# Transposes of batch 1 later in their step, and TensorE's order as written in every chunk

## The chip, the cores and the metric

The kernel runs on one core of a Trainium2 chip. The metric is the device time of one execution in microseconds (us), as the median of several runs. A change within 0.3% of the time before, some 3 us, is about what repeated runs cannot tell from no change.

## The reference, cut to what matters

Attention with a window of 32 positions (half of the heads plain, half with dilation 4) is followed by a rank-32 mix over the sequence and a two-layer ReLU network, each with a residual.

```python
scores = scale * np.matmul(q, k.transpose(0, 1, 3, 2))      # q, k, v: (8, 8, 576, 64)
scores = np.where(masks[None], scores, -1e9)
attn = np.exp(scores - np.max(scores, axis=-1, keepdims=True))
attn = attn / (np.sum(attn, axis=-1, keepdims=True) + 1e-09)
x = np.matmul(attn, v).transpose(0, 2, 1, 3).reshape(8, 576, 512)
...
h = x.transpose(0, 2, 1) @ U @ V                            # rank 32
u = x + h.transpose(0, 2, 1)
return u + np.maximum(u @ w_ch1, 0.0) @ w_ch2               # 512 -> 2048 -> 512
```

## The kernel before, in words

The 4608 tokens are 36 tiles of 128. The two-layer network runs over twelve *chunks* of tiles: chunk 0 has four tiles, chunk 1 two, chunks 2 to 11 three each. In a chunk a loop runs over 16 *units* f, each a 128-wide part of the hidden layer. `layer1(f)` (L853) multiplies the split weights `w1h`, `w1l` with the split inputs `uth`, `utl` into the PSUM tile `ph`, 12 matmuls; ScalarE takes `hh` out of it with the ReLU (L858), VectorE takes the remainder `hl` (L859). `layer2(f)` (L877) adds `hh` times `w2h`, `hh` times `w2l` and `hl` times `w2h` into one `acc` per tile, and runs one unit behind: layer1(f), layer2(f-1), layer1(f+1), ... In the last unit layer2(14) and layer2(15) follow each other. At a chunk's end VectorE adds `acc` to `x` (L913), and `out` is stored.

The attention of the batches is woven into this. A batch has nine *groups* g (batch 1 has g = 9 to 17, the last batch ends with g = 71), and each is a *step*: `pre` multiplies the probabilities of g-2 with v (`product`, tile `pv`, L402), makes the scores of g (`scores`, tiles `s`, L362) and normalizes `pv` into `x` or `xp` on VectorE (`place`, L432). Then come four `soften` (mask and maximum on VectorE, L373; exponential on ScalarE, L377). `post` transposes the probabilities (`turn`): for g < 18 with four TensorE transposes into the PSUM tile `ptp` (L382) and a VectorE copy into `pt` (L388), for the later ones with eight VectorE transposes (L394). `product` issues 8 instructions and `scores` 8; each shows as two passes in the trace, so 16 and 16. After a batch follow `t_rest` (tile `t`, L482) and five `mix_rest` (tile `m`, L504). The tiles `s`, `pv`, `ptp`, `t` and `m` share three PSUM buffers (tag `ps`), given out in the order of the code, so `ptp`, which follows `pv`, `s`, `s`, takes the buffer of that step's `pv` and waits until `place` has read it.

When each piece is issued is set by `queue`: pairs of a position (in units of three tiles) and a call; `slot()`, called after every few matmuls of the network, issues whatever is due. Batch 1 is due in chunk 0, where the weights are also unpacked from 64-bit values (`weight_step`, on all engines but TensorE).

What order the engines then get is another matter. Through chunk 0, and again from the last unit of chunk 11, the block `order = tc.manual_schedule(engines=ORDERED)` keeps all five engines in the order of the code. In between a scheduler with a time model of its own chooses each engine's order, and it may move any instruction ahead of one that it expects to wait.

Of the kernel before, what the change touches and what calls it, by code (L numbers as in the profile page):

```python
# [81 lines left out]
STEP0 = 0.012  # L82
STEP1 = 0.075
SPREAD_AT = 0.5
AFTER = (0.86, 0.90, 0.98, 1.02, 1.06, 1.10, 1.14)
LO2 = 1.31
HI2 = 2.45
# [50 lines left out]
def attention_moe_kernel(ctx: ExitStack, tc: tile.TileContext, qk, vv, masks, ident, ut, vt, uv, w1, w2, out):  # L138
# [196 lines left out]
    def load_v(g, i):  # L335
        if (g, 1, i) in loaded:
            return
        if g < NGB:
            t = early.tile([P, 2, UNITS, VW], F32, tag="v0", name=f"v{g}", bufs=NGB)
            nc.sync.dma_start(out=t, in_=vv[g])  # L340
            loaded[g, 1, 0] = t[:, 0]
            loaded[g, 1, 1] = t[:, 1]
        else:
            t = work.tile([P, UNITS, VW], F32, tag="v", name=f"v{g}_{i}", bufs=4)
            nc.sync.dma_start(out=t, in_=vv[g][:, i])
            loaded[g, 1, i] = t
# [240 lines left out]
    def attention_steps(b):  # L587
        held = {}
        turned = set()
        attn = []  # L590
        for s in range(NGB + LAG):
            g = NGB * b + s

            def pre(s=s, g=g):
                if b >= SPLIT and 0 < s <= NGB:
                    load_v(g - 1, 0)
                    load_v(g - 1, 1)
                if s < NGB and g + 2 < (NGB * SPLIT if b < SPLIT else NG):
                    load_q(g + 2)
                if s >= LAG:  # L600
                    pv = product(g - LAG, held.pop(g - LAG))
                if s < NGB:
                    scores(g)
                if s >= LAG:
                    place(g - LAG, pv)
                if b < SPLIT and LAG <= s < NGB:
                    load_v(g, 0)
                    load_v(g, 1)

            def post(s=s, g=g):  # L610
                late = g - (NGB * b < PE_T)
                if late in state and late not in turned:
                    turned.add(late)
                    held[late] = turn(late, state.pop(late)[0])

            units = [lambda u=u, g=g: soften(g, u) for u in range(UNITS if s < NGB else 0)]
            if b < SPLIT:
                attn.append([lambda pre=pre, units=units, post=post: (pre(), [x() for x in units], post())])
            else:
                attn.append([pre] + units + [post])  # L620
        return attn
# [111 lines left out]
    def batch_items(b):  # L733
        attn = attention_steps(b)
        n = len(batch_parts(b))
        after = [lambda: t_rest(b), lambda: t_sum(b)] + [lambda i=i: mix_rest(b, i) for i in range(n)]
        if b < SPLIT:
            timed = [(STEP0 + STEP1 * i, x) for i, step in enumerate(attn) for x in step]
            timed += [(STEP0 + STEP1 * (i + SPREAD_AT), lambda g=NGB * b + i - LAG: g in scatter and spread_rows(g))
                      for i in range(LAG, len(attn))]  # L740
            timed += list(zip(AFTER, after))
            return sorted(timed, key=lambda e: e[0])
        timed = []
        for i, step in enumerate(attn):
            timed += [(i, step[0])] + [(i + UNIT0 + (UNIT1 - UNIT0) * u / len(step[1:-1]), x) for u, x in enumerate(step[1:-1])] + [(i + POST_AT, step[-1])]
        timed += [(len(attn) + m * TAIL, x) for m, x in enumerate(after)]
        end = len(attn) + len(after) * TAIL
        return [(t / end, x) for t, x in sorted(timed, key=lambda e: e[0])]
# [43 lines left out]
    def after_first():  # L792
        early_open.close()
        make_w(F_MID, F_LAST, None)
# [34 lines left out]
    for c, tiles in enumerate(CHUNKS):  # L829
        slots = [0]  # L830
        nt = len(tiles)
        uh, ul = (e[:, :, 0:nt * P] for e in uts.pop(c))
        acc = [psum.tile([P, DM], F32, tag="acc" if i < CT else "ph", name=f"acc{c}_{i}", bufs=3 if i < CT else 2)
               for i in range(nt)]
        ht = {}

        def slot():
            pos = (tiles[0] + nt * slots[0] / ((nt + 3) * FC - 3)) / CT
            slots[0] += 1
            while queue and queue[0][0] <= pos:  # L840
                queue.pop(0)[1]()

        def layer1(f):
            assert place_of[f, 0] in finished
            ph = psum.tile([P, CTOK], F32, tag="ph", name=f"ph{c}_{f}", bufs=2)[:, 0:nt * P]
            w1h, w1l = held_w[f][0:2]
            ks = (2, 3, 0, 1) if c == f == 0 else range(KC)
            terms = [(w1h, uh), (w1l, uh), (w1h, ul)]
            if c == 0 and f > 0:
                terms = [terms[0], terms[2], terms[1]]  # L850
            seq = [(w, u, k) for w, u in terms for k in ks]
            for n, (w, u, k) in enumerate(seq):
                nc.tensor.matmul(ph, lhsT=w[:, k, :], rhs=u[:, k, :], start=(n == 0), stop=(n == len(seq) - 1))  # L853
                if n % KC == KC - 1 and n < len(seq) - 1:
                    slot()
            hh = work.tile([P, CTOK], F32R, tag="hh", name=f"hh{c}_{f}", bufs=2)[:, 0:nt * P]
            hl = work.tile([P, CTOK], F32R, tag="hl", name=f"hl{c}_{f}", bufs=2)[:, 0:nt * P]
            nc.scalar.activation(out=hh, in_=ph, func=AF.Relu)  # L858
            nc.vector.scalar_tensor_tensor(out=hl, in0=ph, scalar=0.0, in1=hh.bitcast(F32),  # L859
                                           op0=ALU.max, op1=ALU.subtract)  # L860
            ht[f] = (hh, hl)

        def layer2(f):
            assert place_of[f, 1] in finished
            hh, hl = ht.pop(f)
            w2h, w2l = held_w[f][2:4]
            terms = [(hh, w2h), (hh, w2l), (hl, w2h)]
            seq = [(i, n, term) for i in range(nt) for n, term in enumerate(terms)]
            if c == 0:
                terms = [terms[0], terms[2], terms[1]]  # L870
                seq = [(i, n, term) for n, term in enumerate(terms) for i in range(nt)]
            every = slice(0, DM)
            seq = [e + (every,) for e in seq]
            if c == NCHUNK - 1 and f == FC - 1:
                seq[-3:] = [e[:3] + (slice(k * HALF_D, (k + 1) * HALF_D),) for k in range(2) for e in seq[-3:]]
            for m, (i, n, (h, w), cs) in enumerate(seq):
                nc.tensor.matmul(acc[i][:, cs], lhsT=h[:, i * P:(i + 1) * P], rhs=w[:, cs],  # L877
                                 start=(f == 0 and n == 0), stop=(f == FC - 1 and n == 2 and cs.stop == DM))
                if f < FC - 1 and m % 3 == 2 and m < len(seq) - 1:
                    slot()  # L880

        more = list(CHUNKS[c + 1]) if c + 1 < NCHUNK else []
        for f in range(FC):
            if c == 0 and f == F_MID - 1:
                after_first()
            if c == 0:
                weight_step()
            if c == NCHUNK - 1 and f == FC - 1:
                order = tc.manual_schedule(engines=ORDERED)
                order.__enter__()  # L890
            layer1(f)
            if f < FC - 1:
                slot()
            else:
                for t in more[0:2]:
                    transp(t)
            if c == 0:
                weight_step()
            if f > 0:
                layer2(f - 1)  # L900
                if f < FC - 1:
                    slot()
        for t in more[2:]:
            transp(t)
        layer2(FC - 1)
        if c == 0:
            order.__exit__(None, None, None)
        for i, t in enumerate(tiles):
            x = xt.pop(t)
            n = 2 if t == NTILE - 1 else 1  # L910
            for h in range(n):
                cs = slice(h * DM // n, (h + 1) * DM // n)
                nc.vector.tensor_tensor(out=x[:, cs], in0=acc[i][:, cs], in1=x[:, cs], op=ALU.add)  # L913
                nc.sync.dma_start(out=out[t * P:(t + 1) * P, cs], in_=x[:, cs])
        if c == NCHUNK - 1:
            order.__exit__(None, None, None)


def lay_out(q, k, v, U, V, w1, w2):
# [74 lines left out]
```

## Time and profile before

| | |
|---|---|
| runs, median (lowest to highest) | 993.83 us (991.52 to 993.94) |
| profiled execution | 995.63 us |
| its span, first to last instruction | 993.8 us |
| granted TensorE clock, mean over the span | 0.993 |
| TensorE busy | 970.6 us |
| VectorE / ScalarE / GpSimd busy | 501.1 / 267.8 / 73.9 us |

The span is what the trace covers; 1.8 us lie around it. The profiled execution is itself 1.8 us above the median of the three runs. Busy time of TensorE counts from a matmul's start to its modelled end, and matmuls overlap, so that what a matmul costs is read from start to start.

### The profile page before, as it was taken

What the parts mean: (1) busy time and instruction counts of PE and PEld (TensorE: products, weight loads), DVE (VectorE), ACT (ScalarE), POOL (GpSimd) and SP (SyncE); (2) the same over time, 40 slices, a digit from 0 to 9 for tenths busy, and PEclk for the clock granted to TensorE, in tenths of its full rate; (3) what the DMA queues carried; (4) which work ended last, traced back from release to release, by engine and by line L of the source; (5) the groups of instructions that cost most, each with busy time, mean ns of one, the idle gap of its engine ahead of it and who ended that gap; (6) DMA issues with size and microseconds to landing.
All of it is one profiled execution on the core that took longest, in us unless ns stands there. A gap on an engine that the chain in (4) does not pass through costs nothing.

```text
span 993.8 us, 17434 instructions
## 1 busy us (share of the span) xinstructions
PE 970.6 (98%) x6672; PEld 815.3 (82%) x6672; DVE 501.1 (50%) x1686; ACT 267.8 (27%) x669; POOL 73.9 (7%) x67
## 2 busy tenths in 40 slices
PE   8968899999999999999999999999999999999998
PEld 5656677888888888888888888888888888999997
DVE  5646776664657446563356634664536644211211
ACT  7645563221222213222122212221212311111110
POOL 1544453000000000000000000000000000000000
PEclk9979999999999999999999999999999999999999
DMA  9556545322334132321323312332313303100000
GB/s 327 184 181 207 164 155 158 115 79 67 89 95 119 45 76 86 114 74 33 85 72 102 101 27 71 104 112 63 86 40 95 97 11 83 56 1 1 33 1 32
DMA packets 76995, 90.44 MB, mean 91 GB/s; under 512 B 9904, under 2 KB 55280, under 8 KB 76912
## 3 DMA queue, kind: packets, MB, share of 16 engines
q1 hardware_dynamic: 76912, 89.32, 30.1%
q8 instruction: 53, 0.87, 0.4%
q14 instruction: 30, 0.25, 0.1%
HBM read 67.26 MB, written 17.89 MB: 86 GB/s over the span
## 4 chain that ended last, share of the span: by engine, by line
PE 91%; DVE 3%; issue 2%; POOL 2%; DMA 1%; ACT 1%; SPq 0%; DVEq 0%; POOLq 0%
PE ph L853 39%; PE acc L877 39%; PE pv L402 5%; PE s L362 4%; PE t L482 1%; DVE v L204 1%; PE ptp L382 1%; PE m L504 1%; POOL v L204 1%; DMA k<-qk 1%; POOL w1l L211 1%; POOL w2l L211 0%; ACT hh L858 0%; DMA zd<-z 0%; DMA spare<-xp 0%
## 5 line engine op out<-in xcount | busy, mean ns | idle before, releaser
L859 DVE SCALAR_TENSOR_TENSOR hl<-ph,hh 128x384 fp32r<-128x384 f32 (+2 forms) x192 | 106.7, 556 | 269.1 <-ACT hh L858 267.5
L877 PE MATMUL acc<-w2h,hh 128*128 128x512 f32 x577 | 225.3, 403 | 0.6 <-ACT raw L198 0.6
L858 ACT ACTIVATE hh<-ph 128x384 fp32r<-128x384 f32 (+2 forms) x192 | 94.0, 490 | 480.6 <-PE ph L853 473.5
L877 PE MATMUL acc<-w2l,hh 128*128 128x512 f32 x577 | 220.5, 395 | 0.0
L877 PE MATMUL acc<-w2h,hl 128*128 128x512 f32 x577 | 209.4, 397 | 0.0
L853 PE MATMUL ph<-uth,w1h 128*128 128x384 f32 (+2 forms) x768 | 171.0, 342 | 1.3 <-DVE hl L859 1.3
L853 PE MATMUL ph<-uth,w1l 128*128 128x384 f32 (+2 forms) x768 | 167.4, 339 | 0.0
L853 PE MATMUL ph<-utl,w1h 128*128 128x384 f32 (+2 forms) x768 | 166.1, 338 | 0.0
L853 PEld LDWEIGHTS ph<-uth,w1h 128*128 128x128 f32 x768 | 136.4, 189 | 21.5 <-DVE hl L859 2.2
L394 DVE STREAM_TRANSPOSE pt<-p 32x128 f32<-32x128 f32 x432 | 130.4, 302 | 36.9 <-ACT p L377 31.4
L853 PEld LDWEIGHTS ph<-utl,w1h 128*128 128x128 f32 x768 | 134.8, 189 | 3.6
L853 PEld LDWEIGHTS ph<-uth,w1l 128*128 128x128 f32 x768 | 133.1, 188 | 4.7
L377 ACT ACTIVATE p<-p,nmax 128x96 f32<-128x96 f32 x288 | 86.0, 365 | 172.9 <-DVE nmax L373 172.7
L877 PEld LDWEIGHTS acc<-w2h,hh 128*128 128x128 f32 x577 | 108.0, 188 | 24.9 <-issue 1.2
L877 PEld LDWEIGHTS acc<-w2h,hl 128*128 128x128 f32 x577 | 108.0, 189 | 23.8
L877 PEld LDWEIGHTS acc<-w2l,hh 128*128 128x128 f32 x577 | 109.4, 190 | 17.2 <-issue 0.4
L373 DVE CUSTOM_DVE_ANT_0 p<-s,mask 128x96 f32<-128x96 f32 x288 | 57.5, 251 | 26.6 <-PE s L362 26.1
L402 PEld LDWEIGHTS pv<-v,pt 96*64 96x64 f32 x1152 | 44.2, 137 | 30.0 <-issue 26.7
L402 PE MATMUL pv<-v,pt 96*64 96x65 f32 x1152 | 59.0, 230 | 0.0
L362 PE MATMUL s<-k 64*64 64x96 f32 x1152 | 49.1, 256 | 2.1 <-DMA k<-qk 1.0
L362 PEld LDWEIGHTS s<-k 64*64 64x64 f32 x1152 | 31.3, 132 | 17.7 <-issue 11.3
L408 DVE TENSOR_SCALAR ssum<-pv 128x4 f32<-128x4 f32 x72 | 11.3, 157 | 60.3 <-PE pv L402 60.1
(69 smaller groups left out, 494.4 us busy)
## 6 DMA issues: line engine op xcount, KB each, us to landing
k<-qk SPq DMA_DIRECT2D x64, 288.0 KB, 3.2
v<-vv SPq DMA_DIRECT2D x126, 130.0 KB, 2.2
raw<-w SPq DMA_DIRECT2D x25, 512.0 KB, 3.9
out<-x SPq DMA_DIRECT2D x35, 256.0 KB, 2.2
zd<-z SPq DMA_DIRECT2D x120, 64.0 KB, 1.9
xt<-zd SPq DMA_DIRECT2D x30, 256.0 KB, 2.8
raw<-w SPq DMA_DIRECT2D x14, 256.0 KB, 3.1
x<-xp SPq DMA_DIRECT2D x84, 32.0 KB, 1.9
```

Of the source, the lines that this page charges most:

```text
L204: eng.tensor_tensor(out=vi[:, cs], in0=vi[:, cs], in1=lo, op=ALU.add)
L211: eng.tensor_tensor(out=l, in0=v, in1=h.bitcast(F32), op=ALU.subtract)
L362: nc.tensor.matmul(sp[r][i * QB:(i + 1) * QB, a, :], lhsT=qk_sb[rs, a, i * QB:(i + 1) * QB], rhs=qk_sb[rs, a, P + i * off:P + i * off + KB ...
L373: nc.vector.tensor_tensor_reduce(out=p_sb[:, u], in0=sp[u % 2][:, u // 2], in1=mask_sb[:, kind], scale=-1.0 / 8.0, scalar=3.0e38, op0=ALU. ...
L377: nc.scalar.activation(out=p_sb[:, u], in_=p_sb[:, u], func=AF.Exp, bias=nmax[:, u:u + 1], scale=-1.0)
L394: nc.vector.transpose(out=pt[ks, :, rs], in_=p_sb[rs, :, ks])
L402: nc.tensor.matmul(pv[rs, u, :], lhsT=pt[:, u, rs], rhs=loaded[g, 1, i][0:KB, u, :], start=True, stop=True)
L408: nc.vector.tensor_scalar(out=ssum, in0=pv[:, :, D], scalar1=1e-9, scalar2=None, op0=ALU.add)
L853: nc.tensor.matmul(ph, lhsT=w[:, k, :], rhs=u[:, k, :], start=(n == 0), stop=(n == len(seq) - 1))
L858: nc.scalar.activation(out=hh, in_=ph, func=AF.Relu)
L859: nc.vector.scalar_tensor_tensor(out=hl, in0=ph, scalar=0.0, in1=hh.bitcast(F32), op0=ALU.max, op1=ALU.subtract)
L877: nc.tensor.matmul(acc[i][:, cs], lhsT=h[:, i * P:(i + 1) * P], rhs=w[:, cs], start=(f == 0 and n == 0), stop=(f == FC - 1 and n == 2 and ...
```

## The change

Two things change. In batches 0 and 1 (in effect batch 1) a step is no longer one call that issues `pre`, `soften` and `post` together: `post`, with the four transposes and their copy, is due 0.4 of a step later than the rest. And from the end of chunk 0 to the end of the kernel TensorE alone keeps the order of the code, in a second `manual_schedule` block; VectorE, ScalarE and the DMA queue are still left to the scheduler there, and get another order in places since TensorE's is another.

```diff
+BACK_AT = 0.4
...
             if b < SPLIT:
-                attn.append([lambda pre=pre, units=units, post=post: (pre(), [x() for x in units], post())])
+                attn.append([lambda pre=pre, units=units: (pre(), [x() for x in units]), post])
...
-            timed = [(STEP0 + STEP1 * i, x) for i, step in enumerate(attn) for x in step]
+            timed = [(STEP0 + STEP1 * (i + BACK_AT * n), x) for i, step in enumerate(attn) for n, x in enumerate(step)]
...
         if c == 0:
             order.__exit__(None, None, None)
+            bursts = tc.manual_schedule(engines={mybir.EngineType.PE})
+            bursts.__enter__()
...
         if c == NCHUNK - 1:
             order.__exit__(None, None, None)
+            bursts.__exit__(None, None, None)
```

Names in the rows below carry the group, chunk or unit first (`s36`: scores of group 36; `acc3_0`, `hh3_13`: tile 0 of chunk 3, unit 13 of chunk 3) and a running number last.

TensorE in chunk 0, at the transposes of group 11, in the kernel before:

```order
L362 MATMUL s12_0_919<-k12_727 64x96 x2
L362 MATMUL s12_1_920<-k12_727 64x96 x2
L362 MATMUL s12_0_919<-k12_727 64x96 x2
L362 MATMUL s12_1_920<-k12_727 64x96 x2
L382 MATMUL ptp11_948<-id_sb_72,p11_829 96x128 x4
L877 MATMUL acc0_3_625<-w2h_0_83,hh0_2_788 128x512
L877 MATMUL acc0_0_622<-w2h_0_83,hl0_2_789 128x512
```

and in the changed one:

```order
L363 MATMUL s12_0_919<-k12_727 64x96 x2
L363 MATMUL s12_1_920<-k12_727 64x96 x2
L363 MATMUL s12_0_919<-k12_727 64x96 x2
L363 MATMUL s12_1_920<-k12_727 64x96 x2
L878 MATMUL acc0_3_625<-w2h_0_83,hh0_2_788 128x512
L878 MATMUL acc0_0_622<-w2h_0_83,hl0_2_789 128x512
L878 MATMUL acc0_1_623<-w2h_0_83,hl0_2_789 128x512
L878 MATMUL acc0_2_624<-w2h_0_83,hl0_2_789 128x512
L878 MATMUL acc0_3_625<-w2h_0_83,hl0_2_789 128x512
L878 MATMUL acc0_0_622<-w2l_0_84,hh0_2_788 128x512
L383 MATMUL ptp11_956<-id_sb_72,p11_829 96x128 x4
L878 MATMUL acc0_1_623<-w2l_0_84,hh0_2_788 128x512
```

Six matmuls of 512 columns now stand between the scores of group 12 and the transposes of group 11, where none stood.

TensorE near the end of chunk 3, at the scores of group 36, before:

```order
L853 MATMUL ph3_14_4186<-utl3_3548,w1h_13_1697 128x384 x4
L362 MATMUL s36_0_4208<-k36_3688 64x96
L877 MATMUL acc3_0_3587<-w2h_13_1699,hh3_13_4173 128x512
L877 MATMUL acc3_0_3587<-w2l_13_1700,hh3_13_4173 128x512
L362 MATMUL s36_1_4209<-k36_3688 64x96
L877 MATMUL acc3_0_3587<-w2h_13_1699,hl3_13_4174 128x512
L362 MATMUL s36_1_4209<-k36_3688 64x96
L362 MATMUL s36_0_4208<-k36_3688 64x96 x2
L362 MATMUL s36_1_4209<-k36_3688 64x96 x2
L877 MATMUL acc3_1_3588<-w2h_13_1699,hh3_13_4173 128x512
```

and after:

```order
L854 MATMUL ph3_14_4188<-utl3_3550,w1h_13_1697 128x384 x4
L878 MATMUL acc3_0_3589<-w2h_13_1699,hh3_13_4175 128x512
L878 MATMUL acc3_0_3589<-w2l_13_1700,hh3_13_4175 128x512
L878 MATMUL acc3_0_3589<-w2h_13_1699,hl3_13_4176 128x512
L363 MATMUL s36_0_4210<-k36_3690 64x96 x2
L363 MATMUL s36_1_4211<-k36_3690 64x96 x2
L363 MATMUL s36_0_4210<-k36_3690 64x96 x2
L363 MATMUL s36_1_4211<-k36_3690 64x96 x2
L878 MATMUL acc3_1_3590<-w2h_13_1699,hh3_13_4175 128x512
```

The eight matmuls of the scores stood in three pieces here (and one more stood 25 rows earlier, behind the first layer of unit 12); now they stand together, behind the three matmuls of `acc3_0`.

TensorE at the passage from chunk 3 to chunk 4, before:

```order
L853 MATMUL ph4_0_4294<-uth4_4247,w1h_0_81 128x384 x2
L877 MATMUL acc3_0_3587<-w2h_13_1699,hh3_15_4243 128x512
L877 MATMUL acc3_0_3587<-w2l_13_1700,hh3_15_4243 128x512
L877 MATMUL acc3_1_3588<-w2h_13_1699,hh3_15_4243 128x512
L877 MATMUL acc3_1_3588<-w2l_13_1700,hh3_15_4243 128x512
L877 MATMUL acc3_2_3589<-w2h_13_1699,hh3_15_4243 128x512
L877 MATMUL acc3_2_3589<-w2l_13_1700,hh3_15_4243 128x512
L853 MATMUL ph4_0_4294<-uth4_4247,w1h_0_81 128x384 x2
L853 MATMUL ph4_0_4294<-uth4_4247,w1l_0_82 128x384 x3
L877 MATMUL acc3_0_3587<-w2h_13_1699,hl3_15_4244 128x512
```

and after:

```order
L878 MATMUL acc3_2_3591<-w2h_13_1699,hl3_14_4202 128x512
L878 MATMUL acc3_0_3589<-w2h_13_1699,hh3_15_4245 128x512
L878 MATMUL acc3_0_3589<-w2l_13_1700,hh3_15_4245 128x512
L878 MATMUL acc3_0_3589<-w2h_13_1699,hl3_15_4246 128x512
L878 MATMUL acc3_1_3590<-w2h_13_1699,hh3_15_4245 128x512
L878 MATMUL acc3_1_3590<-w2l_13_1700,hh3_15_4245 128x512
L878 MATMUL acc3_1_3590<-w2h_13_1699,hl3_15_4246 128x512
L878 MATMUL acc3_2_3591<-w2h_13_1699,hh3_15_4245 128x512
L878 MATMUL acc3_2_3591<-w2l_13_1700,hh3_15_4245 128x512
L878 MATMUL acc3_2_3591<-w2h_13_1699,hl3_15_4246 128x512
L854 MATMUL ph4_0_4296<-uth4_4249,w1h_0_81 128x384 x4
```

The second layer of the last unit stood behind half of chunk 4's first `ph`, its products with `hl` last; now it follows the second layer of unit 14 at once, and the first product with `hl` is its third matmul.

Counted over all of TensorE's order behind chunk 0, the pieces of `pv` and `s` matmuls that stand between matmuls of the network go from 119 to 66: 42 whole bursts (8 `pv`, then 8 `s`), 12 of `pv` alone and 12 of `s` alone. Those of `t` go from 8 to 6. The `m` stand singly or in pairs before, singly after. What is computed, and the count of every instruction, stays the same.

## Rows read from the trace of the kernel before

**Rows 1.** Busy time of each engine by stretch; its first line names the columns.

```profile
core 0: us, PE busy (x) PEld busy (x) DVE busy (x) ACT busy (x) POOL busy (x), PEclk, DMA share, GB/s
...
36.00:165.00 129.00, 113.04 (x728) 87.70 (x725) 84.09 (x215) 67.88 (x155) 64.97 (x55) 0.95 0.55 175
165.00:860.00 695.00, 695.00 (x4870) 588.25 (x4869) 371.79 (x1315) 158.10 (x416) 0.00 (x0) 1.00 0.28 80
...
55.00:62.00 7.00, 5.91 (x17) 4.81 (x18) 2.60 (x14) 2.84 (x7) 2.69 (x2) 0.51 0.66 218
68.70:72.10 3.40, 3.40 (x10) 2.63 (x9) 1.02 (x2) 2.60 (x8) 1.85 (x2) 0.51 0.18 43
92.60:96.00 3.40, 3.40 (x11) 2.80 (x10) 1.20 (x7) 1.17 (x4) 1.35 (x2) 0.50 0.59 161
```

**Rows 2.** Waits of TensorE from 36 to 165 us: total, times, longest.

```profile
PE ptp L382 <- DVE xp L432: 9.6, 4, 5.1
PE ptp L382 <- DVE x L432: 1.9, 2, 1.2
PE ptp L382 <- ACT raw L198: 1.7, 1, 1.7
PE ph L853 <- DVE hl L859: 1.3, 2, 0.9
```

**Rows 3.** TensorE's timeline at the two longest stalls: start, us, instruction, [idle before].

```profile
56.09 1.06 PE L382 MATMUL ptp<-id_sb,p 128*96 128x128 f32 x4 [5.07 <-DVE xp L432]
68.11 0.61 PE L382 MATMUL ptp<-id_sb,p 128*96 128x128 f32 x4 [2.78 <-DVE xp L432]
```

**Rows 4.** VectorE's timeline just ahead of the first of them.

```profile
55.52 0.42 DVE L432 TENSOR_TENSOR xp<-pv,ssum 128x256 f32<-128x256 f32 x1
```

**Rows 5.** TensorE's timeline around an undivided burst.

```profile
273.81 0.39 PE L877 MATMUL acc<-w2h,hl 128*128 128x512 f32 x1
274.13 0.69 PE L402 MATMUL pv<-v,pt 96*64 96x65 f32 x16
274.75 0.56 PE L362 MATMUL s<-k 64*64 64x96 f32 x16
275.24 0.96 PE L853 MATMUL ph<-uth,w1h 128*128 128x384 f32 x4
```

**Rows 6.** TensorE's timeline around three pieces: the first, one midway, the last.

```profile
166.55 0.64 PE L853 MATMUL ph<-uth,w1h 128*128 128x256 f32 x4
167.11 0.55 PE L362 MATMUL s<-k 64*64 64x96 f32 x8
167.59 0.62 PE L853 MATMUL ph<-uth,w1l 128*128 128x256 f32 x3
...
266.45 0.86 PE L853 MATMUL ph<-utl,w1h 128*128 128x384 f32 x4
267.24 0.56 PE L362 MATMUL s<-k 64*64 64x96 f32 x16
267.73 0.50 PE L877 MATMUL acc<-w2h,hh 128*128 128x512 f32 x1
...
811.61 0.68 PE L853 MATMUL ph<-utl,w1h 128*128 128x384 f32 x3
812.22 0.69 PE L402 MATMUL pv<-v,pt 96*64 96x65 f32 x16
812.84 0.50 PE L877 MATMUL acc<-w2h,hh 128*128 128x512 f32 x1
813.18 0.40 PE L877 MATMUL acc<-w2l,hh 128*128 128x512 f32 x1
```

**Rows 7.** TensorE's timeline at the end of chunk 3.

```profile
380.37 0.39 PE L877 MATMUL acc<-w2h,hh 128*128 128x512 f32 x1
380.60 0.40 PE L877 MATMUL acc<-w2l,hh 128*128 128x512 f32 x1
```

**Rows 8.** VectorE's timeline there.

```profile
382.65 0.55 DVE L859 SCALAR_TENSOR_TENSOR hl<-ph,hh 128x384 fp32r<-128x384 f32 x1
```

## The prediction

> **What bounds the kernel now.** I read the busy time by stretch first. From 165 to 860 us, chunks 1 to 9, TensorE is busy for 695.00 of 695 us at the full clock [rows 1], and the view of waits shows no wait of TensorE at all in that stretch. So there the time is the sum of what TensorE issues, from start to start, and nothing else counts. Chunk 0 is different: between 36 and 165 us TensorE is busy for 113.04 of 129 us, and VectorE for 84.09 [rows 1]. The waits of that stretch name one instruction: the transposes `ptp` stand idle for 9.6 + 1.9 + 1.7 = 13.2 us, mostly for the `xp` or `x` that `place` writes on VectorE [rows 2]. The two longest are 5.07 and 2.78 us [rows 3]; in the first, `place` ends at 55.52 + 0.42 = 55.94 and `ptp` starts at 56.09 [rows 3, 4]. The clock is at its lower level, 1.2 GHz (0.51, 0.51, 0.50 granted), in three stretches, each begun behind one of these stalls: about 6.8, 3.4 and 3.4 us [rows 1].
>
> **What a piece of attention costs between wide matmuls.** Two 512-column matmuls start 0.23 us apart [rows 7]; by the ratio of columns that is 0.17 for 384 and 0.115 for 256. An undivided burst of 16 `pv` and 16 `s` passes lies between the matmul at 273.81 and the one at 275.24: 1.43, less the 0.23 that the first takes anyway, is 1.20 us [rows 5]. The matmul behind a piece is also late in being followed: 813.18 - 812.84 = 0.34 instead of 0.23, 0.11 more [rows 6]. I add it to every piece: a whole burst is 1.31. `pv` alone: 812.84 - 811.61 - 3 x 0.17 = 0.71, with the 0.11 0.82 us. The 16 `s` passes alone: 267.73 - 266.45 - 4 x 0.17 = 0.59, so 0.70. Half of them: 167.59 - 166.55 - 4 x 0.115 = 0.58, so 0.69 [rows 6]. That last pair carries the argument. Eight passes cost as much as sixteen: what is paid for is the change from wide matmuls to small ones and back.
>
> **The change part by part: order behind chunk 0.** Read in this way from start to start, the 119 pieces of `pv` and `s` (the first and the last stand in [rows 6]) add up to 96.7 us. In the changed order there are 66: 42 whole bursts, 12 of `pv` alone and 12 of `s` alone, 42 x 1.31 + 12 x 0.82 + 12 x 0.70 = 55.0 + 9.8 + 8.4 = 73.2 us. That is 23.5 us less. Two cuts fewer in `t`, at the 0.69 of a half piece, are 1.4. The `m` are wide themselves and cost no more in pairs than singly. **First term: -24.9 us.** Its bounds are narrow, 23 to 26, if nothing has to wait in the new order.
>
> The Trainium skill, in TensorEngine Tiling (Array Packing), section Tiling Modes, says that a change of tiling mode drains the array, and TensorE: Matmul & The Clock Gate, Part 2, gives that drain as about 128 cycles. By these an estimate for a cut is two drains, 0.11 us, and 55 cuts fewer would give 6 us where the rows give 24.9; the rows decide.
>
> **New waits behind chunk 0.** The scheduler moved pieces forward and `hl` products back where its model expected a wait, and that cover is gone. Where does it matter? Inside a chunk `hl` of a unit has a whole `ph` and a whole `acc` of matmuls to get ready, some 4.1 us. At a chunk's end layer2(15) follows layer2(14) at once. In chunk 3 `acc` of unit 14 starts at 380.37; nine matmuls and two more at 0.23 bring the first `hl` product to 382.90, and `hl` is written until 382.65 + 0.55 = 383.20 [rows 7, 8]: a wait of 0.3 us, since three subtractions for the next chunk's inputs stand ahead of `hl` on VectorE. Behind that matmul everything on TensorE waits. Of the ten passages between chunks 1 to 11, two have a batch's `t` in between; eight at 0.3 are 2.4 us. In the new VectorE order the first `hl` of the next chunk stands behind the three additions of L913 and six or eight transposes, which I price the same again. **Second term: +5 us**, bounds 0 and 10. The stores and loads that change places on SP's queue wait for nothing that TensorE needs within a step (DMA share 0.28 [rows 1]), and cost nothing; the cover is that each load is issued one or two steps ahead of its use.
>
> **Chunk 0.** Each `post` now comes 6 to 12 wide matmuls behind its scores. At the two longest stalls it is six, 6 x 0.23 = 1.4 us of work done within the stall. The other five stalls are together 13.2 - 5.07 - 2.78 = 5.4 us, each no longer than the work put ahead of it, so they vanish. **Third term: -(1.4 + 1.4 + 5.4) = -8.2 us.** It is not the whole 13.2: the first two stalls keep some 5 us. Bounds: 4, if what `place` waits for on VectorE (which follows unpacking work there) hangs on TensorE only in part, and 13.2.
>
> **Clock.** Matmuls in the second and third slow stretch take twice as long, so each of these costs 1.7 us [rows 1]. Their stalls fall to 1.4 and nothing, and I take both stretches as gone. The first keeps its stall of 3.7 us, and I leave it. **Fourth term: -3.4 us**, bounds 0 and -6.8.
>
> **What the later `post` costs.** Eight times `ptp` becomes a piece of its own. Its joint with the scores is not in the trace; the nearest rows are `pv` and `s` apart, 0.82 + 0.70, against 1.31 together: 0.2 us. **Fifth term: +1.6 us**, bounds 0 and 5.5 (a whole half piece, 0.69). On VectorE the copy into `pt` now stands up to three unpacking instructions later; `product` needs it 0.6 of a step later, and what hides it is the 9 to 15 wide matmuls in between. `post` issues no DMA and passes nothing on SP's or POOL's queue.
>
> **Sum:** -24.9 + 5 - 8.2 - 3.4 + 1.6 = -29.9 us, about 30. The profiled execution took 995.63, the median of the runs 1.8 less; from the median, 993.83 - 29.9 is 964, from the profiled one 966. I say 965.
>
> **The rivals.** (a) Chunk 0 gives nothing: VectorE's unpacking paces it, and time won on TensorE is waited for at the next `place` or `hl`. For it: VectorE is busy 84 of 129 us and keeps its own order. Against it: TensorE's wait for `hl` is only 1.3 us [rows 2]. Then -24.9 + 5 + 1.6: 976. (b) Chunk 0 gives all its 13.2 us and 6.8 of clock, with waits behind it of 2: -24.9 - 13.2 - 6.8 + 2 + 1.6 = -41, 953. (c) A piece's price is time in which TensorE would have waited anyway for `hl`; the scheduler filled waits, and they come back when the pieces are merged. Then the first term is nothing: +5 - 8.2 - 3.4 + 1.6 = -5, 989. Against it: pieces of one kind cost the same to within 0.02 us wherever they stand, and a wait would vary.
>
> The Trainium skill speaks for (c), in TensorE: Matmul & The Clock Gate, Part 2, where weight loads are pulled ahead of matmuls in flight: by that a small piece between wide matmuls hides its loads, cuts are free and the first term is nothing. The trace does not agree: a half piece costs 0.69 us like a whole one [rows 6].
>
> (d) Slower: in program order TensorE stops at the `hl` product of every unit. Behind chunk 0 there are 176 units; to eat the 30 us and 3 more each would wait 0.19 us, and for that `hl`, with 4.1 us of matmuls as its cover, would have to come more than 4.3 us behind its `ph`. VectorE's share of 371.79 of 695 us [rows 1] speaks against it; batch 2, woven into short units of two tiles, is where it could begin. It would give 997 or more. That the change does not do what it says is excluded by the order.
>
> **How the numbers follow.** The forecast of 965 has 0.62, with 956 to 974 from the bounds of its terms; (a) 0.15, (b) 0.12, (c) 0.07, (d) 0.04. From 952 to 980 holds all of the forecast, (a) and most of (b); (c) and (d) stay outside. Within 0.3% of before means within 3 us, which repeated runs could not tell from no change: half of (c) might end there. Faster 0.92, same 0.04, slower 0.04.
>
> **What would show it right or wrong.** From the end of chunk 0 to the end the trace should be some 20 us shorter, whole bursts at 1.3 us each, with TensorE waiting for `hl` of units 15 and 0 at the passages for 2 to 10 us in sum and hardly elsewhere. In chunk 0 the waits at `ptp` should fall from 13.2 to about 5, with the one at the second `ptp` of the chunk the longest, and one slow stretch of the clock be left, not three. The forecast is wrong if waits for `hl` or `pt` stand in most units, if TensorE's wait in chunk 0 moves to `pv` (copy too late) or to `ph`, or if a whole burst costs more than 1.31.

## The result and the profile after

| | before | after |
|---|---|---|
| runs, median (lowest to highest) | 993.83 us (991.52 to 993.94) | 970.34 us (969.68 to 971.48) |
| profiled execution | 995.63 us | 969.68 us |
| its span | 993.8 us | 967.9 us |
| first matmul of chunk 1 starts at | 166.55 us | 156.04 us |
| from there to the end of the span | 827.3 us | 811.9 us |
| granted TensorE clock, mean | 0.993 | 1.0 |

The changed kernel takes 0.9773 of the time before (95%: 0.9746 to 0.9799). The forecast was 965. The last two lines of times split the gain of the span, 25.9 us: 10.5 lie in front of the first matmul of chunk 1, 15.4 behind it. The forecast had some 10 and some 20. The profiled execution is the fastest of the three; the granted clock of the other two, as a mean over the span, was 0.996 and 0.997.

Windows of the trace after, the two stretches that answer to the first two of [rows 1], with the same columns:

```profile
36.00:155.00 119.00, 107.35 (x717) 82.88 (x716) 82.87 (x208) 66.39 (x153) 64.94 (x54) 1.00 0.61 190
155.00:850.00 695.00, 689.64 (x4958) 594.96 (x4957) 379.37 (x1325) 159.55 (x422) 0.00 (x0) 1.00 0.29 81
```

The clock column is at 1.00 throughout chunk 0, so the three slow stretches of before are gone in this execution. Behind chunk 0 TensorE, busy for all of 695 us before, now stands idle for 695 - 689.64 = 5.4 us. The waits of TensorE from 36 to 155 us and, behind "...", from there to the end (the view names what is waited for, the total, the times and the longest):

```profile
PE ptp L383 <- DVE xp L433: 4.2, 2, 3.0
PE pv L403 <- DVE pt L389: 3.1, 2, 1.8
PE ph L854 <- DVE hl L860: 2.0, 2, 1.3
PE s L363 <- DVE x L507: 1.5, 1, 1.5
...
PE acc L878 <- DVE hl L860: 5.1, 9, 1.2
```

In [rows 2] the transposes `ptp` waited 13.2 us in all; now it is 4.2. But `pv` waits for the copy `pt` for 3.1, which it never did before, and `ph` and `s` wait for 2.0 and 1.5, where they waited 1.3 and 0.4. Behind the first stretch one wait is new, for `hl`, 5.1 us in nine pieces. TensorE's timeline at the two `ptp` that still wait, around an undivided burst, and at the end of chunk 3:

```profile
55.50 0.61 PE L383 MATMUL ptp<-id_sb,p 128*96 128x128 f32 x4 [3.03 <-DVE xp L433]
63.49 0.62 PE L383 MATMUL ptp<-id_sb,p 128*96 128x128 f32 x4 [1.22 <-DVE xp L433]
...
273.04 0.39 PE L878 MATMUL acc<-w2h,hl 128*128 128x512 f32 x1
...
274.46 0.96 PE L854 MATMUL ph<-uth,w1h 128*128 128x384 f32 x4
...
365.48 0.39 PE L878 MATMUL acc<-w2l,hh 128*128 128x512 f32 x1
366.19 0.50 PE L878 MATMUL acc<-w2h,hl 128*128 128x512 f32 x1 [0.33 <-DVE hl L860]
366.53 0.40 PE L878 MATMUL acc<-w2h,hh 128*128 128x512 f32 x1
```

A burst lies between 273.04 and 274.46, 1.42 us where [rows 5] had 1.43. At 365.48 two matmuls stand 0.71 us apart instead of the 0.23 of [rows 7], and 0.34 the next two. VectorE's timeline at that place:

```profile
361.24 2.51 DVE L395 STREAM_TRANSPOSE pt<-p 32x128 f32<-32x128 f32 x8 [0.71 <-ACT p L378]
363.78 1.89 DVE L586 TENSOR_TENSOR utl<-xt,uth 128x512 fp32r<-128x512 f32 x3
365.59 0.55 DVE L860 SCALAR_TENSOR_TENSOR hl<-ph,hh 128x384 fp32r<-128x384 f32 x1
```

`hl` of unit 15, 365.59 to 366.14, stands behind three subtractions of 0.63 us and eight transposes, as the prediction read it in chunk 3 of the kernel before [rows 8].

### The profile page after: what moved, and what is told of

It reads as the page before. It is cut to its first block, busy times and chain, and to the rows that moved or that the text cites. A ratio compares the mean times of both kernels' runs of the same rounds, so it can differ in the third digit from the quotient of the medians.

```text
span 967.9 us, 17406 instructions
## 1 busy us (share of the span) xinstructions
PE 945.1 (98%) x6672; PEld 803.1 (83%) x6672; DVE 504.7 (52%) x1686; ACT 266.3 (28%) x669; POOL 73.9 (8%) x67
## 4 chain that ended last, share of the span: by engine, by line
PE 84%; DVE 5%; issue 2%; ACT 2%; DMA 2%; POOL 2%; SPq 1%; DVEq 0%; POOLq 0%
PE acc L878 37%; PE ph L854 36%; PE pv L403 4%; PE s L363 3%; DVE pt L395 1%; ACT p L378 1%; PE t L483 1%; POOL v L205 1%; DVE v L205 1%; PE m L505 1%; DMA raw<-w 1%; PE ptp L383 1%; POOL w1l L212 1%; DVE hl L860 1%; PE idle_ps L766 1%
## 5 line engine op out<-in xcount | busy, mean ns | idle before, releaser
L878 PE MATMUL acc<-w2h,hl 128*128 128x512 f32 x577 | 220.6, 394 | 5.2 <-DVE hl L860 5.1
L878 PE MATMUL acc<-w2h,hh 128*128 128x512 f32 x577 | 222.2, 398 | 0.8 <-ACT raw L199 0.6
L854 PE MATMUL ph<-uth,w1h 128*128 128x384 f32 (+2 forms) x768 | 168.4, 340 | 2.0 <-DVE hl L860 2.0
L878 PEld LDWEIGHTS acc<-w2h,hl 128*128 128x128 f32 x577 | 108.0, 188 | 34.3 <-DVE hl L860 11.2
L374 DVE CUSTOM_DVE_ANT_0 p<-s,mask 128x96 f32<-128x96 f32 x288 | 57.0, 251 | 12.1 <-PE s L363 11.4
L403 PEld LDWEIGHTS pv<-v,pt 96*64 96x64 f32 x1152 | 39.4, 137 | 24.7 <-issue 18.4
L403 PE MATMUL pv<-v,pt 96*64 96x65 f32 x1152 | 49.4, 227 | 3.1 <-DVE pt L389 3.1
L363 PE MATMUL s<-k 64*64 64x96 f32 x1152 | 41.7, 257 | 1.6 <-DVE x L507 1.5
L363 PEld LDWEIGHTS s<-k 64*64 64x64 f32 x1152 | 27.6, 133 | 11.8 <-issue 5.6
```

The lines of the kernel that those rows point to most:

```text
L363: nc.tensor.matmul(sp[r][i * QB:(i + 1) * QB, a, :], lhsT=qk_sb[rs, a, i * QB:(i + 1) * QB], rhs=qk_sb[rs, a, P + i * off:P + i * off + KB ...
L374: nc.vector.tensor_tensor_reduce(out=p_sb[:, u], in0=sp[u % 2][:, u // 2], in1=mask_sb[:, kind], scale=-1.0 / 8.0, scalar=3.0e38, op0=ALU. ...
L403: nc.tensor.matmul(pv[rs, u, :], lhsT=pt[:, u, rs], rhs=loaded[g, 1, i][0:KB, u, :], start=True, stop=True)
```

## The experiments

Every kernel below starts from the changed one. First the times (median of the runs, ratio to the kernel before with its 95% interval, and the two parts of the profiled span):

| | us | ratio | chunk 1 starts at | behind it |
|---|---|---|---|---|
| before | 993.83 | | 166.55 | 827.3 |
| after | 970.34 | 0.9746 to 0.9799 | 156.04 | 811.9 |
| bursts alone | 977.82 | 0.982 to 0.9861 | 164.72 | 811.9 |
| later transposes alone | 986.53 | 0.9915 to 0.996 | 158.18 | 827.3 |
| `hl` products last in units 0 and 15 | 961.82 | 0.9668 to 0.9702 | 156.17 | 803.2 |
| `pv` apart from its scores | 982.47 | 0.9872 to 0.9918 | 158.72 | 823.1 |
| VectorE in program order too | 970.00 | 0.9742 to 0.9776 | 154.45 | 812.3 |
| `pt` copied by ScalarE | 967.24 | 0.9719 to 0.9748 | 153.22 | 811.5 |
| transposes 0.7 of a step later | 974.49 | 0.9778 to 0.9829 | 161.44 | 811.8 |
| transposes 0.2 of a step later | 973.23 | 0.978 to 0.982 | 159.36 | 811.8 |
| `w2h` written by ScalarE | 961.35 | 0.9661 to 0.9693 | 147.65 | 811.4 |
| `hl` last, `pt` by ScalarE | 959.86 | 0.9642 to 0.9671 | 154.56 | 803.2 |
| these two and `w2h` by ScalarE | 952.30 | 0.9569 to 0.9601 | 147.30 | 803.3 |

Kernels that share an order behind chunk 0 repeat that part to within 0.5 us.

**Bursts alone.**

```diff
-BACK_AT = 0.4
+BACK_AT = 0.0
```

> TensorE in program order behind chunk 0, but the transposes of batch 1 due with their scores as before (0.0 of a step). Theory: the two parts add up, and behind chunk 0 the gain is cuts (49 pieces fewer, 25.0 us by their start-to-start prices in the two traces) less waits for hl at the passages between chunks (9.7 us from start to start). Chunk 0 stays at 133 us as before, chunks 1 to 11 lose 15: a span of 978 to 979, and the 13 us of waits at ptp and the slow clock stretches of chunk 0 are all back. Rival: the gain of the whole change is mostly chunk 0's waits and clock, and the cuts are free: 988 or more.

977.82 us, and a span of 976.6 in the profile, near the theory's 978 to 979. Behind chunk 0 nothing differs from the changed kernel, 811.9 us; chunk 0 is as long as in the kernel before but for 1.8 us, `ptp` waits 9.6 + 1.9 + 1.7 us again, and the slow stretches of the clock are back (0.992 granted over the span). The 49 pieces are another count than the change's own: they take in `t` and `m` and go from 151 to 102, where 53 pieces of `pv` and `s` and two of `t` fall away and six of `m` are added.

**Later transposes alone.**

```diff
-            bursts = tc.manual_schedule(engines={mybir.EngineType.PE})
-            bursts.__enter__()
...
-            bursts.__exit__(None, None, None)
```

> The other half alone: transposes of batch 1 due 0.4 of a step later, TensorE's order behind chunk 0 left to the scheduler. Theory: chunk 0 is 9.9 us shorter as in the changed kernel, chunks 1 to 11 as before with 151 pieces: a span of 983 to 985. Rival: half of chunk 0's gain is only lent, since batch 2 and the scheduler's order behind it start from the same VectorE backlog: 988 or more.

986.53 us, and a span of 985.5 in the profile, at the upper end of the theory. Behind chunk 0 the time is that of the kernel before, 827.3 us; ahead of it 8.4 us are gained. The two halves gain 16.0 and 7.3 us, together 23.3 of the 23.5 that the whole change gains: they touch different stretches and do not help each other. That chunk 0's part is 7.3 to 8.4 where the changed kernel's trace shows 10.5 is the scatter of chunk 0: kernels with the same code there start chunk 1 at 156.04 (changed), 156.17 and 154.45 (two that follow), while this one and the one with `pv` apart start it at 158.18 and 158.72. Part of this scatter is the clock. The last two have two slow stretches of 3.4 us each in chunk 0, the one at 156.17 has one, and the other two have none. The first of them in this kernel, with the stall ahead of it:

```profile
55.26 1.06 PE L383 MATMUL ptp<-id_sb,p 128*96 128x128 f32 x4 [3.06 <-DVE xp L433]
...
54.00:62.00 8.00, 6.74 (x52) 5.39 (x53) 4.10 (x17) 4.61 (x10) 2.93 (x3) 0.79 0.69 230
```

**`hl` products last.** In units 0 and 15, behind chunk 0, `layer2` now runs through all tiles with the two products of `hh` before it comes to that of `hl`.

```diff
                 seq = [(i, n, term) for n, term in enumerate(terms) for i in range(nt)]
+            elif f == 0 or (f == FC - 1 and c < NCHUNK - 1):
+                seq = [(i, n, term) for n, term in enumerate(terms) for i in range(nt)]
```

> The changed kernel with another order inside the second layer of units 0 and 15 of chunks 1 to 11 (unit 15 of chunk 11 excepted): first hh times w2h of all tiles, then hh times w2l, then hl times w2h, so that the first product with hl is the 7th matmul and no longer the 3rd, 0.9 us later. Theory: the 9.7 us between the forecast by cuts (25.0) and the measured gain behind chunk 0 (15.3) are short waits for hl at these units, each under 1.3 us; nearly all go, and the span falls by 7 to 9 to about 960. Rival: VectorE is late there as a whole, and the wait moves to the next thing TensorE needs of it (hl of unit 1, or PSUM): 966 to 968.

961.82 us. The waits of TensorE behind 156 us:

```profile
PE acc L880 <- ACT hh L859: 0.2, 1, 0.2
```

The pieces of `pv` and `s` cost what they did, 73 us in both kernels read from start to start, so the gain is not theirs. No wait for `hl` is shown any more, and that part of the span is 811.9 - 803.2 = 8.7 us shorter, though the view had put down 5.1 us to these waits. So they cost more than it shows. The rows at 365.48 above say how: the view has 0.33 us there, counted from the modelled end of the matmul before; from start to start it is (0.71 - 0.23) + (0.34 - 0.23) = 0.59 us. At the ends of chunks 2, 5, 8, 9 and 10 the same product starts some 0.17 us late, and its follower 0.11, with next to no idle time in the view. Read in this way, the changed kernel's waits for `hl` are 3.0 us in the last units of eight chunks and 5.9 us in the first units of six, 8.9 in all.

**`pv` apart from its scores.** From batch 2 on, the scores of a step come due 0.2 of a step behind `pv`; what `product` and `scores` issue is unchanged.

```diff
+REST_AT = 0.2
...
-            timed += [(i, step[0])] + [(i + UNIT0 + (UNIT1 - UNIT0) * u / len(step[1:-1]), x) for u, x in enumerate(step[1:-1])] + [(i + POST_AT, step[-1])]
+            units = step[2:-1]
+            timed += [(i, step[0]), (i + REST_AT, step[1])]
+            timed += [(i + UNIT0 + (UNIT1 - UNIT0) * u / len(units), x) for u, x in enumerate(units)] + [(i + POST_AT, step[-1])]
```

> The changed kernel with the scores due 0.2 of a step behind the product with v from batch 2 on: 141 pieces for 102, nothing else moved on purpose. Theory: a cut has a price wherever it is; 39 cuts at 0.82 + 0.70 - 1.31 = 0.21 us are 8 us, a span of 975 to 977, with no new waits. Rival (weight loads hide behind the wide matmuls): cuts are free, 967 to 969.

982.47 us, 12.1 more than the changed kernel; in the traces 823.1 - 811.9 = 11.2 us lie behind chunk 0, and 2.7 are the scatter of chunk 0. TensorE's timeline at one of the cuts:

```profile
270.14 0.86 PE L862 MATMUL ph<-utl,w1h 128*128 128x384 f32 x4
270.93 0.69 PE L404 MATMUL pv<-v,pt 96*64 96x65 f32 x16
271.54 0.50 PE L886 MATMUL acc<-w2h,hh 128*128 128x512 f32 x1
271.88 0.40 PE L886 MATMUL acc<-w2l,hh 128*128 128x512 f32 x1
272.11 0.40 PE L886 MATMUL acc<-w2h,hl 128*128 128x512 f32 x1
272.44 0.56 PE L364 MATMUL s<-k 64*64 64x96 f32 x16
272.93 0.50 PE L886 MATMUL acc<-w2h,hh 128*128 128x512 f32 x1
```

`pv` alone: 271.54 - 270.14 - 4 x 0.17 + 0.11 (0.34 behind it instead of 0.23) = 0.83; `s` alone: 272.93 - 272.11 - 0.23 + 0.11 = 0.70. These are the prices of the prediction, 0.82 and 0.70 against 1.31 together. A cut is 0.21, and 39 of the 42 bursts are cut, 8.2 us: cuts are not free. The time still missed the 975 to 977, which had no new waits in it. The other 3 us are mostly wait: that for `hl` rises from 5.1 to 8.3 us:

```profile
PE acc L886 <- DVE hl L868: 8.3, 10, 1.7
```

**VectorE in program order too.**

```diff
-            bursts = tc.manual_schedule(engines={mybir.EngineType.PE})
+            bursts = tc.manual_schedule(engines={mybir.EngineType.PE, mybir.EngineType.DVE})
```

> VectorE keeps program order too behind chunk 0, so hl stands ahead of the next chunk's subtractions and of half of the batch's score reductions. Theory A: hl of units 15 and 0 is late because of what stands ahead of it in VectorE's queue. Then most of the 9.7 us of hl waits go, some 6 of them: 964 us. Theory B: hl is late by its own chain, ph to hh to hl, whatever stands ahead: 970, with the same waits for hl. Theory C: what hl is moved past (the subtractions, the reductions) is what TensorE needs next, and the waits move there, to ph and pv: 970 to 975, with other names in the view of waits.

970.00 us, the same. Its waits behind chunk 0:

```profile
PE m L505 <- DVE ts_sb L496: 4.1, 5, 1.3
PE ph L854 <- DVE utl L586: 2.4, 2, 1.2
PE acc L878 <- DVE hl L860: 0.5, 3, 0.2
```

Theory C: the waits for `hl` shrink to 0.5 us, so it was what stands ahead of `hl` in VectorE's queue that made it late, but the wait goes to `m` and `ph`, whose inputs `ts_sb` and `utl` are now the late ones. Doing the products in another order on TensorE removed the wait; reordering VectorE only renamed it.

**`pt` copied by ScalarE.**

```diff
-            nc.vector.tensor_copy(out=pt, in_=turn_pe(g, p_sb))
+            nc.scalar.copy(out=pt, in_=turn_pe(g, p_sb))
```

> The copy of the transposed probabilities in chunk 0 is written by ScalarE in place of VectorE; nothing else of the change is touched. Theory A: the new waits of pv for pt, 3.1 us, come from the copy's place behind unpacking work in VectorE's queue. Then they go, VectorE has some 8 x 0.6 us less to do, and chunk 0 is 3 to 5 us shorter: 966 us. Theory B: VectorE's unpacking and softening pace chunk 0 as a whole and what one wait gives up the next one (ptp, s, ph) takes: 969 to 971.

967.24 us, 3.1 us less. Waits of TensorE, 36 to 165 us:

```profile
PE ptp L383 <- DVE xp L433: 3.1, 2, 1.6
...
PE pv L403 <- ACT pt L389: 1.4, 1, 1.4
```

`pv` and `ptp` give 1.7 and 1.1 us. Theory A in its direction; half of the wait of `pv` stays. The gain is near the scatter of chunk 0: VectorE in program order, with the copy still on VectorE, started chunk 1 at 154.45, this kernel at 153.22.

**The distance, 0.7 and 0.2 of a step.** One constant, `BACK_AT`, in each.

> The back part of a step comes 0.7 of a step behind its scores instead of 0.4. Theory A (each stall stands alone, and a later place removes it): the waits at ptp fall from 4.2 us to under 1, those of pv for pt stay at some 3: 967 us. Theory B (VectorE paces chunk 0, and the distance only moves the waits): ptp gives 3 us, pv and s take 3 or more, since pt now has 0.3 of a step to be copied: 970 to 973.

> The back part of a step comes 0.2 of a step behind its scores instead of 0.4: some three wide matmuls in place of six. Theory A (a stall is covered by the matmuls put into it, and the copy into pt has 0.8 of a step before pv needs it): the waits at ptp are some 0.7 us longer each than with 0.4, some 7 to 9 us in all where the changed kernel has 4.2, those of pv for pt vanish, and one or two slow stretches of the clock come back: 971 to 975. Theory B (VectorE paces chunk 0, the place on TensorE matters little): 968 to 971.

974.49 and 973.23 us. With 0.7 no `ptp` waits any more, and `pv` waits for its copy; with 0.2 it is the reverse (waits of 36 to 165 us and of the whole span):

```profile
PE pv L403 <- DVE pt L389: 11.1, 6, 2.8
```

```profile
PE ptp L383 <- DVE xp L433: 6.3, 3, 4.2
...
PE ptp L383 <- ACT raw L199: 1.1, 1, 1.1
```

So the place on TensorE does matter (theory A for 0.2), but `ptp` and `pv` share the room of a step, as theory B had it: what one is given the other lacks, at 0.7 by far more than the 3 us expected. All waits of TensorE from 36 to 165 us add up to 10.8 us with 0.2, 11.6 with 0.4 and 13.6 with 0.7, and the mean granted clock of the three profiled executions is 0.994, 1.0 and 0.994; what 0.2 loses to 0.4 is seen in the clock, not in the waits. 0.4 lies near the best of the four distances (0: 977.82, 0.2: 973.23, 0.4: 970.34, 0.7: 974.49). With 0.2 the first stall is 4.17 us and TensorE's clock falls behind it:

```profile
54.00:62.00 8.00, 6.78 (x20) 5.49 (x21) 2.73 (x14) 2.83 (x7) 2.70 (x2) 0.57 0.70 232
```

**`w2h` written by ScalarE.** In chunk 0's unpacking, 15 of the 16 roundings of `w2` leave VectorE.

```diff
-            narrow_c(v, h, l, nc.gpsimd, layer == 0 and f > 0)
+            narrow_c(v, h, l, nc.gpsimd, f > 0)
```

> The rounded copy of w2 in chunk 0's unpacking (16 casts of 0.42 us, in front of which VectorE also waits 3.8 us for GpSimd) is written by ScalarE. TensorE's order is that of the changed kernel. Theory A: what TensorE still waits for in chunk 0 (ptp, pv, s, ph: 10.8 us in all) is late because unpacking stands ahead of it in VectorE's queue; with 10 us less there, half of these waits go: 964 to 966. Theory B: the unpacking itself (GpSimd's part, the transfers of the raw weights) paces chunk 0, or ScalarE, now with some 16 x 0.6 us more, delays hh and p by as much: 969 to 972.

961.35 us, 9.0 less, more than theory A's most: chunk 1 starts 8.4 us earlier. Waits of TensorE:

```profile
PE pv L403 <- DVE pt L389: 1.4, 2, 1.1
PE ph L854 <- DVE hl L860: 1.2, 1, 1.2
...
PE ptp L383 <- ACT raw L199: 0.6, 1, 0.6
PE s L363 <- DVE x L507: 0.2, 1, 0.2
```

The transposes' waits for `xp` are gone, and `pv` waits 1.4 instead of 3.1. TensorE's order is untouched, and ScalarE took on 9.3 us without any new wait for `hh` or `p`. So most of what TensorE waited for in chunk 0 was late because of the work in VectorE's queue: the waits of the first list, 10.8 us, are 3.4 here.

**Together.**

> The two edits together: hl products last in units 0 and 15 of chunks 1 to 11, and the copy into pt on ScalarE. If they touch different stretches, as the theory has it, their gains add: 961.8 less what the copy alone gives beside the changed kernel, 3 to 4 us by theory A of that run, 958; 962 by theory B.

> Three edits together on the changed kernel: hl products last in units 0 and 15, the copy into pt and the rounded copy of w2 on ScalarE. The first two gave 959.9. If the third frees VectorE (theory A of its own run), 955 to 957; if it only loads ScalarE, which then also carries the copy into pt, 960 to 963.

959.86 and 952.30 us. The first lies between the expectations of 958 and 962, the second below both of its own. The gains add where the edits touch different stretches: with `hl` last the part behind chunk 0 is 803.2 and 803.3 us here too. They do not add within chunk 0: `hl` last -8.5, `pt` -3.1 and `w2h` -9.0 would make 949.7 from 970.34, 2.6 us less than measured, and chunk 1 starts at 147.30 where `w2h` alone had 147.65. With the roundings gone from VectorE's queue, moving the copy as well gains almost nothing, as it should if both gains come from that one queue. The two longest totals of TensorE's waits in it behind 36 us:

```profile
PE ph L854 <- DVE hl L860: 1.3, 1, 1.3
PE pv L403 <- ACT pt L389: 0.7, 2, 0.4
```

At 0.9585 of the time before (0.9569 to 0.9601) this is the fastest version here.

## Why the prediction was right, and where it was off

The likeliest case came: faster, and 970.34 us lies inside its own 956 to 974. It is 5 us above the 965, and the steps differ more than that.

**First term, the pieces: the size right, its reason only in part.** -24.9 with bounds 23 to 26. With the `hl` waits taken out, the part behind chunk 0 is 827.3 - 803.2 = 24.1 us shorter than before. Cutting the bursts again brought back 0.21 us a cut, as the first term's prices say. Rival (c), that a piece's price is time in which TensorE would have waited anyway, falls with it.

What does not hold is the sentence on which the prediction rests its argument, that eight passes cost as much as sixteen. Two other pieces in the kernel before, each between its neighbours:

```profile
233.25 0.40 PE L877 MATMUL acc<-w2l,hh 128*128 128x512 f32 x1
233.58 0.33 PE L402 MATMUL pv<-v,pt 96*64 96x65 f32 x2
233.84 0.50 PE L877 MATMUL acc<-w2h,hh 128*128 128x512 f32 x1
...
306.94 0.51 PE L853 MATMUL ph<-uth,w1h 128*128 128x384 f32 x2
307.39 0.40 PE L362 MATMUL s<-k 64*64 64x96 f32 x8
307.71 0.73 PE L877 MATMUL acc<-w2h,hl 128*128 128x512 f32 x2
```

Without the 0.11 behind it, two `pv` passes cost 233.84 - 233.25 - 0.23 = 0.36 us, where 16 cost 0.71. Eight `s` passes cost 307.71 - 306.94 - 2 x 0.17 = 0.43, where 16 cost 0.59. The eight that the prediction read, behind 167.11, cost 0.58. There the trace has the passes start two at a time, some 0.08 us apart, so that they need four rounds; in a whole piece they start four at a time and need four rounds as well, and the eight behind 307.39 start four at a time and need two. So a piece has a price of its own, even for two passes, and each round adds to it. The term came out because its 96.7 us had been added up piece by piece from starts, not from that rule.

The Trainium skill says in TensorE: Matmul & The Clock Gate, Part 2, that weight loads are pulled ahead of matmuls in flight. The trace agrees so far as loads go on beside matmuls: they are busy for 588.25 of the 695 us in which TensorE's matmuls are busy throughout [rows 1]. But cuts are not free for that, which is what the prediction had drawn from it for rival (c): the kernel with `pv` apart paid 0.21 us for each.

**Second term, new waits for `hl`: the right waits, too small.** +5 was said, within 0 and 10; 8.7 us went when they were removed. "Eight at 0.3" was near: the last units of eight chunks wait 3.0 us from start to start, where 2.4 were said. At the end of chunk 3 it is 0.59, of which 0.11 is the late follower, which the prediction adds to every piece but to no wait. The step that failed is the sentence that prices the first `hl` of the next chunk the same again: the first units of six chunks wait 5.9 us. The longest of these waits, on TensorE, and the transposes that VectorE does just ahead of `hl`:

```profile
529.91 0.50 PE L878 MATMUL acc<-w2h,hl 128*128 128x512 f32 x1 [1.21 <-DVE hl L860]
...
527.39 1.87 DVE L395 STREAM_TRANSPOSE pt<-p 32x128 f32<-32x128 f32 x6 [0.71 <-ACT p L378]
```

Ahead of `hl` VectorE has four reductions of the scores, a wait of 0.71 us for `p`, and six transposes, 527.39 to 529.26. What the first units wait beyond the forecast is the larger part of the gap between 965 and 970.

**Third term, chunk 0's stalls: overstated.** -8.2 was said; `ptp`'s waits did fall by 9.0 us, to 4.2 at two places (about 5 were forecast), but [rows 2] and the rows after add up to 14.5 and 10.8 us: the net is some -4. What the step missed is the sentence that hid the copy into `pt` behind 9 to 15 wide matmuls. It stands behind unpacking of up to 1.66 us on VectorE, and two `pv` waited 3.1 us for it. The first of them, on VectorE and on TensorE:

```profile
79.76 1.65 DVE L205 CUSTOM_DVE_ANT_0 v<-raw,v 128x1024 uint16<-128x1024 uint16 x1
81.33 0.68 DVE L389 COPY pt<-ptp 96x512 f32<-96x512 f32 x1
...
82.06 0.69 PE L403 MATMUL pv<-v,pt 96*64 96x65 f32 x16 [1.75 <-DVE pt L389]
```

The prediction priced this at nothing, and yet had named a wait that moves to `pv` or `ph` as a sign that it is wrong. By that sign its account of chunk 0 was wrong in part. The `w2h` kernel shows the common cause: rival (a), VectorE's queue paces chunk 0, was half right.

**Fourth term, the clock: more than forecast in this execution, about as forecast in others.** -3.4 was said, with the first slow stretch left. In the profiled execution none is left: behind the stall of 3.03 us at 55.50 the granted clock stays at 1.0 (2.4 GHz):

```profile
54.00:62.00 8.00, 6.50 (x57) 5.09 (x57) 5.43 (x18) 4.58 (x10) 3.97 (x4) 1.00 0.72 243
```

That is luck of this execution. The kernel with later transposes alone has the same code in chunk 0 and the same stall, 3.06 us, and there the clock fell, to a mean of 0.79 over the same eight microseconds. Over the five profiles with this code the slow stretches are none, none, one, two and two, of 3.4 us each, where the kernel before had 13.6 us. The means of the changed kernel's other two runs, 0.996 and 0.997, stand for some 8 and 6 us at half the clock, by an estimate (0.004 x 969.7 x 2 and 0.003 x 968.5 x 2). Longer stalls at the same place, 4.17 us with 0.2 of a step and 5.07 us before [rows 3], were each followed by a slow stretch, and so were one of 2.78 us [rows 3] and one of 1.7 us [rows 2]. So the length of the stall is not all that decides; the rest stays open.

**Fifth term, `ptp` as a piece of its own:** +1.6 was said. It was not measured by itself. What the trace has is the sum: chunk 1 starts 10.5 us earlier, some 4 by waits, 0.6 by an earlier start of chunk 0, and the other 6 by clock and pieces together. With a clock worth at most 6.8, little room is left for the fifth term; its size stays open.

So terms three to five came to -10.5 in this trace, against -10.0 forecast, by errors that cancel and a clock that happened not to fall. By the medians chunk 0's half is worth less, 7.3 us alone and 7.5 on top of the bursts (977.82 - 970.34). Behind chunk 0 the trace has -15.4 against -24.9 + 5 = -19.9, and most of that gap is the second term. The total is off by these two. Rival (b) is out, since chunk 0 kept 10.8 us of waits. Rival (d) is out as well: inside a chunk no unit but the first and the last waits for `hl`.

## What to carry to other kernels

Where TensorE never idles, read the cost of small matmuls between wide ones from start to start, piece by piece: here a piece of two passes cost over half of what one of 16 does, and merging pieces gained the 24 us that those rows said. One pair of equal prices, though, is no rule; look for a third piece. When a scheduler's freedom is taken away, look for what it had been covering, at the passages between stages first, and price a wait by starts too, since the view of waits showed only 5.1 of 8.7 us. When a wait can go away in two places, ask which engine's queue makes both late: moving the transposes back and forth traded `ptp` for `pv`, and taking work out of VectorE's queue removed most of both. Before a gain or a loss of a few microseconds is put down to an edit, look at the granted clock of each run: of five kernels with the same chunk 0, the two where it fell twice started chunk 1 some 2 to 4 us later than the two where it did not fall.

## What was not expected of the hardware

One VectorE instruction, the unpacking at L205 over 1024 elements, takes 1.66 us or 0.69 us. VectorE's and GpSimd's rows around one in the changed kernel:

```profile
60.65 1.40 POOL L212 TENSOR_TENSOR w2l<-v,w2h 128x512 fp32r<-128x512 f32 x1 [0.77 <-DVE w2h L211]
...
60.94 1.66 DVE L205 CUSTOM_DVE_ANT_0 v<-raw,v 128x1024 uint16<-128x1024 uint16 x1
```

and in the kernel with `w2h` on ScalarE:

```profile
57.64 1.85 POOL L212 TENSOR_TENSOR w2l<-v,w2h 128x512 fp32r<-128x512 f32 x1 [0.73 <-ACT w2h L209]
...
57.64 0.69 DVE L205 CUSTOM_DVE_ANT_0 v<-raw,v 128x1024 uint16<-128x1024 uint16 x1
```

In the first GpSimd started at 60.65 and ended at 62.05, and VectorE's instruction, started at 60.94, ended 0.55 us later; of the 0.69 us that it takes elsewhere, most lies behind GpSimd's end. In the second both started at 57.64; VectorE took 0.69 us and GpSimd 1.85 instead of 1.40, 0.45 more. The Trainium skill has this in SBUF — State Buffer, section Who interferes with whom: a VectorE instruction with two inputs in SBUF and a GpSimd one that reads it exclude each other, and the one that starts first holds the other up. These rows agree. It bears on the `w2h` kernel's gain: the eleven such instructions of chunk 0 take 18.2 us in the changed kernel and 12.3 there, while the shifts of L203 rose from 15.1 to 18.0, which leaves VectorE 3 us less work beside the 6.3 us of the 15 roundings. How much of the 9 us comes from this, no run shows by itself.
